# Moving a residual from identity matmuls on TensorE to an addition on VectorE, fed by DMA crossbar transposes

## Chip, cores and metric

The kernel runs on 1 core of one Trainium2 chip. The metric is the device time of one launch in microseconds (us), lower is better. Each time is a median of several executions. Verdicts compare executions of the same state ("fast"); an execution over 1.5% above the fastest of its kernel is called "slow" and left out of a verdict, except where I say otherwise.

## The reference

The input is x, 8 batches of 3136 tokens of 256 channels. A global filter (real FFT over the tokens, product with a complex filter, inverse FFT) is followed by a mixer:

```python
y  = irfft(rfft(x, axis=1) * (filt_r + 1j * filt_i), n=3136, axis=1)
u  = y + (y^T @ U @ V)^T             # low rank (32) over the tokens
out = u + relu(u @ w_ch1) @ w_ch2    # 256 -> 1024 -> 256 channels
```

The change concerns the "u +" of the last line.

## The kernel before

The FFT of length 3136 = 64 x 49 is done as two stages of matmuls each way, in fp16, with intermediate results (ct1, ct2) written to and read from device memory. The batches are worked in five units: 0 and 1 have one batch, 2 to 4 have two. A unit passes through f1 (first stage: x loads, matmul, cast to asb, store to ct1), mid (second stage: a2 loads, matmul pz, filter product uv on VectorE, matmul pe, cast to esb, store to ct2), load_e2, low_rank and then groups of 512 tokens, 6 for each of units 0 and 1 and 12 for each of the others (48), plus one shorter group for each unit. While the groups of one unit run, f1 and mid of the next units are dealt between their steps. Instruction order on each engine is chosen by a scheduler when the kernel is built; each engine and each DMA queue then runs in that order.

A group first makes u with the channels on the partitions (`ut`), because that is what the next matmul needs as its input. The output wants tokens on the partitions, so `ut` must be transposed to be added. Before, this is done by two more matmuls for each 128 tokens, which add into the PSUM tile of the product with w_ch2:

```python
def stage4(gr):
    ...                                        # cut: matmuls into pu
    nc.vector.tensor_copy(gr.ut, pu)           # [128, 2, 512] fp16, channel-major

def residual(gr, o, t0, n):
    for dh in range(2):
        nc.tensor.matmul(o[:, dh * 128:dh * 128 + 128], gr.ut[:, dh, t0:t0 + n], idn,
                         start=False, stop=(dh == 1), skip_group_check=True)

def mm2_part(gr, t):
    ...                                        # cut: the shorter last group
    for tt in range(4 * half, 4 * half + 4):
        nc.tensor.matmul(o, gr.h[tt][:, i * 128:(i + 1) * 128], w2sb[:, tt * DM:(tt + 1) * DM],
                         start=(tt == 0), stop=False, skip_group_check=True)
    if half:
        residual(gr, o, i * 128, 128)
    if t % 4 == 3:
        ...                                    # cut
        nc.vector.tensor_copy(dst, gr.pc.rearrange("p (b j d) -> p b j d", b=u.nb, j=u.jc))

def mirror_filters(a, z):                      # 2 x 808 KB, SBUF to SBUF, at the end of unit 0's mid
    nc.sync.dma_start(fab[0:NR, 1, a:z, :], fab[NR:98, 0, a:z, :])      # NR = 49 partitions
    nc.sync.dma_start(fab[NR:98, 1, a:z, :], fab[0:NR, 0, a:z, :])
```

Loads of x and stores of asb (from unit 1 on) go out on the GpSimd queue, nearly everything else on the sync queue.

## Time and profile before

| | before |
|---|---|
| median of 3 executions | 636.09 us (633.97 to 637.58) |
| span of the profiled execution | 630.4 us |
| PE / VectorE / ScalarE busy | 90% / 51% / 53% |

From the profile's page of the kernel before: busy time of each engine (us, share of the span, instructions), the chain of waits by engine, and the groups of the identity matmuls and of the VectorE copy (busy us, mean ns of one).

```profile
PE 567.5 (90%) x4161; PEld 404.9 (64%) x4161; DVE 323.1 (51%) x376; ACT 332.1 (53%) x618; POOL 83.2 (13%) x136
...
PE 76%; DMA 18%; ACT 2%; SPq 1%; issue 1%; DVE 1%; POOL 0%; ACTq 0%; POOLq 0%
...
L551 DVE COPY och<-pc 128x512 f32<-128x512 f32 x96 | 66.2, 690 | 148.4 <-PE pc L513 131.7
...
L513 PE MATMUL pc<-idn,ut 128*128 128x128 f16 x394 | 55.0, 219 | 0.0
```

The 219 ns are the length of one pipelined matmul, not what it costs. The timeline of PE (start us, length us) shows the cost:

```profile
530.12 0.27 PE L541 MATMUL pc<-w2sb,h_6256 128*128 128x256 f16 x1
530.23 0.28 PE L513 MATMUL pc<-idn,ut 128*128 128x128 f16 x2
530.35 0.60 PE L497 MATMUL phh<-ut,w1sb 128*128 128x512 f16 x2
```

The two identity matmuls start at 530.23 and the next instruction at 530.35, so a pair costs 0.11 to 0.12 us of PE, and a group with its four pairs about 0.44 us.

The next view gives, for stretches of 20 us of the kernel before, the busy us of each engine, then the granted TensorE clock, the busy share of the DMA engines and GB/s.

```profile
80.00:100.00 20.00, 18.64 (x96) 10.55 (x95) 6.72 (x6) 10.57 (x18) 4.82 (x9) 0.79 0.85 193
100.00:120.00 20.00, 15.79 (x120) 11.01 (x119) 9.63 (x13) 9.77 (x19) 9.44 (x16) 1.00 0.98 240
...
160.00:180.00 20.00, 15.90 (x135) 11.09 (x134) 10.78 (x11) 6.96 (x13) 0.00 (x0) 1.00 0.85 218
180.00:200.00 20.00, 19.81 (x116) 12.10 (x115) 17.09 (x15) 13.40 (x25) 0.00 (x0) 1.00 0.65 180
...
560.00:580.00 20.00, 20.00 (x162) 15.32 (x161) 5.91 (x7) 11.60 (x21) 0.00 (x0) 1.00 0.22 59
```

From 80 to 180 us the DMA engines are 85 to 98% busy and PE has gaps. Later PE is full and DMA has room on the whole, but not everywhere: from 240 to 260 us, just before unit 2's groups, the DMA engines are 90% busy again. The chain of waits in the early part runs through transfers (start us, length us):

```profile
109.64 8.58 DMA a_848<-ct_1
...
136.26 13.15 DMA ct_1<-esb
```

### The profile page before, as it was taken

The page shows a single profiled execution, that of the slowest core. Times are in us where ns is not written, and L with a number is a line of the kernel's source. Part 1 is how long each engine was busy: PE and PEld are TensorE (multiplying, and loading weights), DVE is VectorE, ACT ScalarE, POOL GpSimd, SP SyncE. Part 2 cuts the span into 40 slices and gives each one's busy share as a digit, 9 for nine tenths or more (in the row PEclk, how much of TensorE's full clock was granted, in tenths as well). Part 3 has the DMA queues.
Part 4 walks back from the last instruction along what each step waited for, and adds up shares of the span by engine and source line. Part 5 has one row for each costly group of instructions (what it writes and reads, how often), then busy time and mean ns, then how long its engine had stood idle before and what let it go on. Part 6 is the DMA issues. An engine that isn't in the chain of part 4 may idle for free.

```text
span 630.4 us, 10659 instructions
## 1 busy us (share of the span) xinstructions
PE 567.5 (90%) x4161; PEld 404.9 (64%) x4161; DVE 323.1 (51%) x376; ACT 332.1 (53%) x618; POOL 83.2 (13%) x136
## 2 busy tenths in 40 slices
PE   3178289799899999999999999999999999999995
PEld 0166146556556656667677677776777777777774
DVE  5165125676478853337777643476777223233231
ACT  0033046466366656464666665556565555555552
POOL 4230524314100113120001110100000000000000
PEclk9975569999999999999999999999999999999999
DMA  9797689999965579775437685826242753123033
GB/s 164 187 229 185 134 187 220 236 239 218 211 211 154 130 182 285 199 175 144 130 103 174 145 222 190 216 79 185 78 123 75 156 156 101 37 65 101 1 101 109
DMA packets 51993, 98.28 MB, mean 156 GB/s; under 512 B 7386, under 2 KB 29816, under 8 KB 51746
## 3 DMA queue, kind: packets, MB, share of 16 engines
q1 hardware_dynamic: 38742, 69.23, 40.0%
q0 software_dynamic: 11232, 27.20, 21.4%
q10 hardware_dynamic: 1968, 1.17, 0.7%
q8 instruction: 32, 0.52, 0.4%
q14 instruction: 19, 0.16, 0.1%
HBM read 59.88 MB, written 51.38 MB: 177 GB/s over the span
## 4 chain that ended last, share of the span: by engine, by line
PE 76%; DMA 18%; ACT 2%; SPq 1%; issue 1%; DVE 1%; POOL 0%; ACTq 0%; POOLq 0%
PE phh L497 24%; PE pc L541 23%; PE pe L347 8%; PE pz L379 5%; PE pu L482 3%; PE pu L488 3%; PE pc L513 3%; DMA ct_1<-esb 3%; DMA e_2424<-ct_2 3%; PE pf L285 2%; DMA a_342<-ct_0 2%; SPq L420 1%; DMA a_848<-ct_1 1%; DMA a_217<-ct_0 1%; DMA e_540<-ct_0 1%; DMA tf_77<-tf 1%
## 5 line engine op out<-in xcount | busy, mean ns | idle before, releaser
L497 PE MATMUL phh<-ut,w1sb 128*128 128x512 f16 (+2 forms) x848 | 245.8, 369 | 1.8 <-DVE ut L491 1.3
L394 DVE TENSOR_TENSOR uv<-pz,fab 98x1024 f16<-98x1024 f32 (+1 forms) x132 | 141.8, 1087 | 47.6 <-PE pz L379 46.1
L551 DVE COPY och<-pc 128x512 f32<-128x512 f32 x96 | 66.2, 690 | 148.4 <-PE pc L513 131.7
L358 ACT CAST esb<-pe 98x512 f16<-98x512 f32 (+1 forms) x160 | 79.9, 501 | 97.0 <-PE pe L347 78.4
L497 PEld LDWEIGHTS <-w1sb 128*128 128x128 f16 x848 | 105.9, 145 | 31.6 <-issue 8.9
L347 PE MATMUL pe<-uv,g_80 98*98 98x512 f16 (+1 forms) x330 | 90.3, 361 | 1.2 <-DMA g_80<-g 1.2
L491 DVE CAST ut<-pu 128x1024 f16<-128x1024 f32 x48 | 58.7, 1224 | 36.9 <-PE pu L488 36.0
L347 PEld LDWEIGHTS <-g_80 98*98 98x98 f16 x330 | 44.5, 138 | 18.3 <-issue 4.7
L513 PE MATMUL pc<-idn,ut 128*128 128x128 f16 x394 | 55.0, 219 | 0.0
L156 POOL DMA_DIRECT2D x<-in_x_dram x48 | 26.2, 558 | 181.4 <-PE pf L285 169.8
L379 PEld LDWEIGHTS <-tf_77 98*98 98x98 f16 x165 | 22.6, 137 | 32.8 <-issue 21.5
L513 PEld LDWEIGHTS <-ut 128*128 128x128 f16 x394 | 38.5, 98 | 6.8 <-issue 0.8
L290 DVE CAST asb<-pf 128x1024 f16<-128x1024 f32 x21 | 25.6, 1221 | 19.6 <-PE pf L285 18.8
L387 DVE TENSOR_TENSOR uv<-pz,fab 98x512 f16<-98x512 f32 x33 | 22.6, 691 | 12.5 <-PE pz L384 12.1
L285 PE MATMUL pf<-x,wf_64 128*128 128x512 f16 x84 | 25.7, 379 | 0.1
L288 ACT CAST asb<-pf 128x1024 f16<-128x1024 f32 x21 | 21.3, 1012 | 4.7 <-PE pf L285 4.2
L379 PE MATMUL pz<-a_168,tf_77 98*98 98x256 f16 x4 | 1.6, 406 | 14.7 <-DMA a_168<-ct_0 14.3
L433 PEld LDWEIGHTS <-ut_96 128*32 128x32 f16 x120 | 3.1, 101 | 16.0 <-DMA e_537<-ct_0 8.8
L305 POOL DMA_DIRECT2D ct_4<-asb x12 | 8.3, 700 | 36.2 <-ACT asb L288 36.2
L305 POOL DMA_DIRECT2D ct_2<-asb x12 | 8.5, 713 | 29.5 <-ACT esb L358 25.8
L358 ACT ACT_TABLE_LOAD x1 | 1.3, 1283 | 20.2 <-DMA ct_0<-asb 20.2
L285 PEld LDWEIGHTS <-wf_64 128*128 128x128 f16 x84 | 7.4, 98 | 4.3 <-issue 1.6
(1477 smaller groups left out, 1122.3 us busy)
## 6 DMA issues: line engine op xcount, KB each, us to landing
out_dram<-och SPq DMA_DIRECT2D x96, 192.0 KB
x<-in_x_dram POOLq DMA_DIRECT2D x48, 256.0 KB, 7.3
out_dram<-och SPq DMA_DIRECT2D x16, 384.0 KB
ct_2<-asb POOLq DMA_DIRECT2D x12, 256.0 KB, 6.5
ct_3<-asb POOLq DMA_DIRECT2D x12, 256.0 KB, 6.3
ct_4<-asb POOLq DMA_DIRECT2D x12, 256.0 KB, 5.6
ct_2<-esb SPq DMA_DIRECT2D x15, 196.0 KB
ct_3<-esb SPq DMA_DIRECT2D x15, 196.0 KB
```

The lines of the kernel that those rows point to most:

```text
L156: nc.gpsimd.dma_start(t[64 * p:64 * p + 64], dram(x.tensor, (u.b[0] * SEQ + 8 * c) * DM + st * p, [[NR * DM, 64], [1, 8 * DM]]))
L285: nc.tensor.matmul(pf[:, i, :], wf1, u.x[c][:, r:r + 2, :], start=True, stop=True)
L290: nc.vector.tensor_copy(dst, pf)
L347: nc.tensor.matmul(pe[0:98, 0:bd], g3[:, (2 * k + l) * 98:(2 * k + l + 1) * 98], uv[:, l * bd:(l + 1) * bd], start=(k != 32 and l == 0), s ...
L358: nc.scalar.copy(st["esb"][:, i, :], pe[0:98, 0:bd])
L379: nc.tensor.matmul(pz[0:98, 0:bd], wz, a2[c][:, i, :], start=True, stop=True)
L394: nc.vector.tensor_mul(uv.rearrange("p (f b d) -> p f b d", f=2, b=nb), zin, fin)
L491: nc.vector.tensor_copy(gr.ut, pu)
L497: nc.tensor.matmul(ph[:, 0:n], w1v[:, dh, :, t], gr.ut[:, dh, 0:n], start=(dh == 0), stop=(dh == 1))
L513: nc.tensor.matmul(o[:, dh * 128:dh * 128 + 128], gr.ut[:, dh, t0:t0 + n], idn, start=False, stop=(dh == 1), skip_group_check=True)
L541: nc.tensor.matmul(o, gr.h[tt][:, i * 128:(i + 1) * 128], w2sb[:, tt * DM:(tt + 1) * DM], start=(tt == 0), stop=False, skip_group_check=True)
L551: nc.vector.tensor_copy(dst, gr.pc.rearrange("p (b j d) -> p b j d", b=u.nb, j=u.jc))
```

## The change

The intent is to take the identity matmuls off PE, the busiest engine, and to use DMA and VectorE, which have room on average. A crossbar transpose (a DMA that transposes the data on its way) on the sync queue makes a token-major fp16 copy of `ut` (256 KB, SBUF to SBUF), and the VectorE copy out of PSUM, which had to be done anyway, becomes an addition.

```diff
         nc.vector.tensor_copy(gr.ut, pu)
 
+        gr.u16 = sb.tile([128, 2, 4, 128], F16, tag="u16", bufs=2, name="u16")
+        nc.sync.dma_start_transpose(gr.u16.rearrange("p h i d -> p (h i) d"),
+                                    gr.ut.rearrange("p h t -> p (h t)"))
@@ mm2_part
-                             start=(tt == 0), stop=False, skip_group_check=True)
-        if half:
-            residual(gr, o, i * 128, 128)
+                             start=(tt == 0), stop=(tt == 7), skip_group_check=True)
@@ (cut)
-            nc.vector.tensor_copy(dst, gr.pc.rearrange("p (b j d) -> p b j d", b=u.nb, j=u.jc))
+            res = gr.u16[:, :, 2 * y:2 * y + 2, :].rearrange("p h i d -> p i h d")
+            nc.vector.tensor_add(dst.rearrange("p b j (h d) -> p (b j) h d", h=2),
+                                 gr.pc.rearrange("p (i h d) -> p i h d", i=2, h=2), res)
```

## The prediction

> **What bounds the kernel now.** The chain of waits is 76% PE, 18% DMA. The table of stretches splits the span. From 80 to 170 us the 16 DMA engines are 85 to 98% busy and the chain passes through transfers (8.6 us for a2 from ct_1 at 109.6 us, 13.2 us for ct_1 from esb at 136.3). From about 180 us on PE is 98 to 100% busy in nearly every 20 us at clock 1.00, while DMA falls to 13-30% in the last 100 us. Early time is DMA latency, late time is PE issue.
>
> **Removed.** 384 of 394 identity matmuls (the last groups keep theirs). The group list's 219 ns each is pipelined length; in the timeline at 530 to 547 us a pair takes 0.11 us of PE, 0.055 us each: 384 x 0.055 = 21 us; the chain's 3.1% (20 us) agrees. About 50 lie before 180 us, mostly hidden behind DMA; the other 330 are 18 us on the critical path.
>
> **Changed on VectorE.** The 96 copies of 128x512 from PSUM (690 ns) become additions with an SBUF operand. The existing tensor_tensor of 98x512 from PSUM takes 691 ns, so I expect 690 to 720 ns: under 3 us in all, on an engine 51% busy.
>
> **Added.** 48 crossbar transposes of 256 KB, SBUF to SBUF, on the sync queue between the loads and stores that feed the chain. Their source rows are 256 B; packets of 256 B in this trace took 18 ns, so an estimate is 1024 x 18 ns / 16 = 1.2 us of all engines. The Trainium skill, "DMA: Bandwidth & Descriptors", Latency and other measured facts, gives 261 GB/s for a transpose with a non-contiguous middle dimension: estimate 1.0 us. "VectorE: DVE Perf Modes", The three transpose paths, gives 1309 ns for one 128x128 block; eight in series would be 10.5 us, a pessimistic estimate. No trace here shows which yet.
>
> **Deadlines.** stage4 of a group comes every 8.3 us in the tail. Two u16 buffers let a transpose start 1 to 2 us after ut is written; the first addition comes some 11 us later. A landing within 5 us is hidden. In the first unit it is not: the transposes queue behind the two 808 KB mirror copies of the filters (issued 79.8 and 80.8 us), on busy engines. I expect first additions some 3 us later, VectorE, which runs in order, holding back the asb casts, and so a2 loads of unit 1. Seven transposes before 170 us add 8 us of DMA time. Cost early: 5 to 8 us. Later blocking on the sync queue (waits for ut ahead of stores of esb): 2 to 3 us.
>
> **Sum.** 636 - 18 + 7 + 2 = 627, call it 626 us. Range 612 to 648. Faster by over 2% (under 623.4): 0.34; within 2%: 0.47; slower: 0.19.
>
> **What would show each step.** PE: 384 matmuls fewer, and groups in 520 to 620 us every 7.8 to 7.9 us instead of 8.3. VectorE: the addition's mean near 700 ns. DMA: issue to landing of u16 under 5 us in the tail, few waits of och on u16 after 260 us; before 170 us such waits of several us in all. The PE-saturated part starts 5 to 8 us later than before.
>
> **What would make it wrong.** A transpose that takes near 10 us, or stops other traffic while it runs: then additions wait on u16, PE waits for pc, and the result is 650 us or more. The sync queue being held while a transpose is issued, so that a2 and e2 loads come late. Or the opposite: transposes cost nothing in the DMA-bound part, and the whole 20 us comes through (616 us).

## More of the kernel before

A landmark that exists once in each unit is the ScalarE cast of its low-rank sum, after which its groups begin. I use it throughout to cut the span into five stretches: "unit 0 to unit 1" is the time from unit 0's cast to unit 1's, and so on; the last stretch runs to the end. The view is that of the cast's line; "first and last start" is its time.

```profile
L440 ACT CAST h_588<-ph x1: 372/372/372, 79.2 to 79.2; 128x256 f16<-128x256 f32 x1
L440 ACT CAST h_1603<-ph x1: 372/372/372, 174.5 to 174.5; 128x256 f16<-128x256 f32 x1
L440 ACT CAST h_2673<-ph x1: 586/586/586, 257.5 to 257.5; 128x512 f16<-128x512 f32 x1
L440 ACT CAST h_4428<-ph x1: 586/586/586, 387.1 to 387.1; 128x512 f16<-128x512 f32 x1
L440 ACT CAST h_6087<-ph x1: 586/586/586, 513.0 to 513.0; 128x512 f16<-128x512 f32 x1
```

## The result

| | before | after |
|---|---|---|
| median, 4 executions each | 635.98 us | 657.36 us (655.35 to 660.32) |
| ratio | | 1.0342 (95%: 1.029 to 1.0393) |
| span of the profiled execution | 630.4 us | 653.6 us |

A ratio here is the mean time of one kernel's fast runs over that of the other's of the same rounds, so it is not quite the ratio of the medians that I quote. The result is correct, and 3.4% slower; 626 us had been predicted.

The lines of the page after that answer to those shown of before, and a group of the new addition from the list of VectorE's groups:

```profile
PE 555.3 (85%) x3777; PEld 389.8 (60%) x3777; DVE 322.6 (49%) x376; ACT 331.0 (51%) x618; POOL 83.3 (13%) x136
...
PE 70%; DMA 23%; DVE 2%; ACT 2%; SPq 2%; issue 1%; POOL 0%; ACTq 0%; DVEq 0%; POOLq 0%
```

```profile
L554 DVE TENSOR_TENSOR och<-pc,u_1282 128x512 f32<-128x512 f32 x2 | 1.4, 693 | 2.5 <-PE pc L545 2.5
```

PE has 4161 - 3777 = 384 matmuls fewer, as intended, and the addition costs what the copy cost (693 against 690 ns). The loss is elsewhere. The casts of the low-rank sums after:

```profile
L440 ACT CAST h_588<-ph x1: 372/372/372, 79.6 to 79.6; 128x256 f16<-128x256 f32 x1
L440 ACT CAST h_1581<-ph x1: 372/372/372, 205.9 to 205.9; 128x256 f16<-128x256 f32 x1
L440 ACT CAST h_2615<-ph x1: 585/585/585, 287.5 to 287.5; 128x512 f16<-128x512 f32 x1
L440 ACT CAST h_4298<-ph x1: 585/585/585, 419.7 to 419.7; 128x512 f16<-128x512 f32 x1
L440 ACT CAST h_5885<-ph x1: 585/585/585, 543.0 to 543.0; 128x512 f16<-128x512 f32 x1
```

| stretch (us) | before | after | difference | removed matmuls alone would give |
|---|---|---|---|---|
| start to unit 0 | 79.2 | 79.6 | +0.4 | 0 |
| unit 0 to unit 1 | 95.3 | 126.3 | +31.0 | -2.7 |
| unit 1 to unit 2 | 83.0 | 81.6 | -1.4 | -2.7 |
| unit 2 to unit 3 | 129.6 | 132.2 | +2.6 | -5.3 |
| unit 3 to unit 4 | 125.9 | 123.3 | -2.6 | -5.3 |
| unit 4 to end | 117.4 | 110.6 | -6.8 | -5.3 |

(The last column is 0.44 us times 6 or 12 groups.) All of the loss, and more, is in one stretch. In the tail, where PE is full and DMA has room, the change does what it was meant to do: the transposes go out every 7.8 us, while the matmuls of the same place in each group (stage4) came every 8.3 us before. Timeline of PE before, then of the sync queue after:

```profile
530.78 0.39 PE L482 MATMUL pu<-s_78,e_5814 128*128 128x128 f16 x4
...
539.10 0.39 PE L482 MATMUL pu<-s_78,e_5817 128*128 128x128 f16 x4
...
547.41 0.39 PE L482 MATMUL pu<-s_78,e_5817 128*128 128x128 f16 x4
```

```profile
580.45 1.23 SPq L494 DMA_TRANSPOSE u_6307<-ut  x1
...
588.27 1.23 SPq L494 DMA_TRANSPOSE u_6405<-ut  x1
...
596.11 1.23 SPq L494 DMA_TRANSPOSE u_6499<-ut  x1
```

The stretches of 20 us after:

```profile
80.00:100.00 20.00, 16.61 (x96) 10.46 (x96) 6.39 (x7) 12.07 (x19) 5.38 (x10) 0.96 1.07 179
100.00:120.00 20.00, 6.31 (x35) 4.23 (x35) 2.46 (x4) 0.36 (x1) 4.27 (x7) 0.57 1.06 145
...
160.00:180.00 20.00, 16.18 (x93) 11.53 (x92) 8.64 (x12) 9.21 (x22) 5.26 (x10) 0.74 1.04 168
180.00:200.00 20.00, 10.17 (x49) 6.06 (x50) 7.26 (x8) 3.45 (x6) 0.00 (x0) 0.74 0.95 192
...
560.00:580.00 20.00, 20.00 (x158) 15.38 (x157) 7.12 (x9) 11.94 (x20) 0.00 (x0) 1.00 0.47 109
```

From 100 to 120 us PE works 6.3 us in place of 15.8. The DMA engines show more busy time (1.06 in place of 0.98) and move less (145 in place of 240 GB/s): their packets take longer. (The share adds up the time of all packets; packets that overlap can bring it over 1.) PE's granted clock, 1.00 before, is 0.57 and 0.74.

The chain of waits after names a culprit at once, a second one later:

```profile
83.05 29.88 DMA u_607<-ut
112.95 0.70 DVE och L554
...
271.78 15.65 DMA u_2418<-ut
```

The first transpose takes 29.9 us from its issue to the addition that waits for it. VectorE, which runs in order, stands idle for 15.7 us before that addition, and PE behind it, from 98.0 to 113.7 us. VectorE's timeline, the first copy before and the first addition after:

```profile
95.64 0.68 DVE L551 COPY och<-pc 128x512 f32<-128x512 f32 x1
```

```profile
112.95 1.29 DVE L554 TENSOR_TENSOR och<-pc,u_607 128x512 f32<-128x512 f32 x2 [15.74 <-DMA u_607<-ut]
```

And the sync queue is held while it issues transposes (the view of the transpose's line; the middle figure of the three is the ns that an issue took):

```profile
L494 SPq DMA_TRANSPOSE u_607<-ut x1: 7785/7785/7785, 83.0 to 83.0; - x1
L494 SPq DMA_TRANSPOSE u_647<-ut x1: 14947/14947/14947, 91.0 to 91.0; - x1
...
L494 SPq DMA_TRANSPOSE u_1282<-ut x1: 10616/10616/10616, 155.9 to 155.9; - x1
...
L494 SPq DMA_TRANSPOSE u_2418<-ut x1: 10438/10438/10438, 271.8 to 271.8; - x1
...
L494 SPq DMA_TRANSPOSE u_3479<-ut x1: 1232/1232/1232, 361.7 to 361.7; - x1
```

An issue takes 1.2 us in a quiet stretch; of the six in unit 0 to unit 1, four take 5 to 15 us. In the records of single DMA packets, the 1024 pieces of 256 B of one transpose pass within 1.4 us in the tail, the last 2.6 us after the issue began; those of the first are spread over some 20 us. They start at 87.2 us, stop at 89.2 and go on at 98.2, when the mirror copies end. Near the first, eight packets of x loads (4096 B, usually 322 ns) took 10.6 to 11.0 us each, from 88.7 us on; before, no packet of this size took over 2.4 us.

So there are three suspects for one stretch: VectorE standing in order behind a late u16; a crossbar transpose that holds up other transfers; and simply 256 KB more for each group in a place where the DMA engines are full. The chain alone cannot tell, since it follows only the wait that ended last.

### The profile page after: what moved, and what is told of

Read it like the earlier page. It is cut to its first block, busy times and chain, and to the rows that moved or that the text cites. A ratio compares the mean times of both kernels' runs of the same rounds, so it can differ in the third digit from the quotient of the medians.

```text
span 653.6 us, 9996 instructions
## 1 busy us (share of the span) xinstructions
PE 555.3 (85%) x3777; PEld 389.8 (60%) x3777; DVE 322.6 (49%) x376; ACT 331.0 (51%) x618; POOL 83.3 (13%) x136
## 4 chain that ended last, share of the span: by engine, by line
PE 70%; DMA 23%; DVE 2%; ACT 2%; SPq 2%; issue 1%; POOL 0%; ACTq 0%; DVEq 0%; POOLq 0%
PE phh L501 23%; PE pc L545 22%; PE pe L347 8%; PE pz L379 5%; DMA u_607<-ut 5%; PE pu L482 3%; PE pu L488 3%; DMA u_2418<-ut 2%; PE pf L285 2%; DMA a_1167<-ct_1 2%; DMA a_342<-ct_0 2%; DMA ct_1<-esb 1%; DMA a_217<-ct_0 1%; DMA e_540<-ct_0 1%; DMA tf_77<-tf 1%; DMA ct_0<-al 1%
## 5 line engine op out<-in xcount | busy, mean ns | idle before, releaser
L501 PEld LDWEIGHTS <-w1sb 128*128 128x128 f16 x848 | 112.2, 145 | 33.6 <-issue 6.3
L347 PEld LDWEIGHTS <-g_80 98*98 98x98 f16 x330 | 45.4, 140 | 24.9 <-issue 10.4
L379 PEld LDWEIGHTS <-tf_77 98*98 98x98 f16 x165 | 23.4, 142 | 42.7 <-issue 18.3
L545 PE MATMUL pc<-w2sb,h_689 128*128 128x256 f16 x4 | 1.3, 334 | 15.7 <-DVE och L554 15.7
L379 PE MATMUL pz<-a_1597,tf_77 98*98 98x512 f16 x4 | 2.3, 577 | 10.8 <-DMA a_1597<-ct_2 10.8
L318 ACT CAST al<-pf 128x256 f16<-128x256 f32 (+1 forms) x4 | 1.5, 368 | 17.5 <-PE pf L312 17.5
```

Source lines behind the costliest of these rows:

```text
L347: nc.tensor.matmul(pe[0:98, 0:bd], g3[:, (2 * k + l) * 98:(2 * k + l + 1) * 98], uv[:, l * bd:(l + 1) * bd], start=(k != 32 and l == 0), s ...
L379: nc.tensor.matmul(pz[0:98, 0:bd], wz, a2[c][:, i, :], start=True, stop=True)
L501: nc.tensor.matmul(ph[:, 0:n], w1v[:, dh, :, t], gr.ut[:, dh, 0:n], start=(dh == 0), stop=(dh == 1))
```

## The experiments

All ran on one core against the kernel before. "Stretch" below is unit 0 to unit 1 in the run's profile (one execution). In the runs where unit 0 has nothing added this stretch is 95.3, 96.6, 96.6, 97.9, 98.1, 99.4 and 100.9 us, so I take 95 to 101 us as undisturbed. (The 100.9 is from a profile of the slow state, of units 2 to 4 below; without it the range ends at 99.4.) Single profiles scatter elsewhere too: the time before unit 0's cast, which no experiment was to change, is 73.8 to 82.2 us. So I compare stretches, not spans, and in this stretch take no difference under some 5 us in one profile for an effect.

### Transposes that nobody reads

The kernel before with the 48 transposes added:

```diff
         nc.vector.tensor_copy(gr.ut, pu)
+        gr.u16 = sb.tile([128, 2, 4, 128], F16, tag="u16", bufs=2, name="u16")
+        nc.sync.dma_start_transpose(gr.u16.rearrange(...), gr.ut.rearrange(...))
```

> The kernel before (identity matmuls, copies) plus the 48 transposes, whose result nobody reads. Measure: the time from the cast of the low-rank sum of unit 0 to that of unit 1 (95.3 us before, 126.3 us after), and the ratio to before. Theory X (a crossbar transpose that meets busy DMA engines stalls traffic and holds the sync queue): the loss stays without any reader, interval 112 to 128 us, ratio 1.03 to 1.06, with x packets of 4096 B that take over 5 us. Rival S (the loss is VectorE standing in order behind the wait for u16): interval under 103 us, ratio under 1.015.

Measured: correct, 672.12 us (one of the four executions slow), ratio 1.0585 (1.0537 to 1.0633); stretch 126.6 us, against 126.3 with the reader. VectorE's timeline in this run:

```profile
96.03 0.68 DVE L555 COPY och<-pc 128x512 f32<-128x512 f32 x1
...
101.16 0.69 DVE L555 COPY och<-pc 128x512 f32<-128x512 f32 x1 [1.45 <-PE pc L517]
...
112.17 1.22 DVE L290 CAST asb<-pf 128x1024 f16<-128x1024 f32 x1 [7.07 <-DMA ct<-asb]
```

The first two copies out of PSUM come at 96.0 and 101.2 us (95.6 and 100.8 before), so VectorE no longer waits for a transpose. It is held at 112.2 us all the same, by a store of asb that is late, and the chain now runs through x loads, stores of ct and loads of a2:

```profile
122.11 15.47 DMA a<-ct
```

Rival S falls as the whole cause: taking away the 15.7 us wait that stood on the chain gives back nothing, so the loss needs no reader. It does not follow that the wait was harmless in the kernel after, since the two equal stretches are made up differently. PE's long gap is from 98.0 to 113.7 us there, behind the addition, and from 119.0 to 137.6 us here, until loads of a2 land. The first matmul pz of unit 1 starts 34.7 us after unit 0's cast before, 47.2 after and 58.2 here; the rest of the stretch is 60.6, 79.1 and 68.4 us.

### A plain copy in the place of the transpose, read

```diff
-        nc.sync.dma_start_transpose(gr.u16.rearrange("p h i d -> p (h i) d"),
-                                    gr.ut.rearrange("p h t -> p (h t)"))
+        nc.sync.dma_start(gr.u16.rearrange("p h i d -> p (h i) d")[:, :, 0:128],
+                          gr.ut.rearrange("p h (i d) -> p (h i) d", d=128))   # u16 rows padded to 144
```

> The kernel after with each transpose replaced by a plain copy of the same 256 KB on the same queue, at the same place, written in runs of 256 B, read by the same additions. The result is wrong on purpose. Theory X (it is the crossbar transpose's own behaviour under load): interval unit 0 to unit 1 back to 96 to 106 us, no x packet over 5 us, sync queue held about 0.6 us an issue, ratio to before 0.965 to 0.995. Rival Q (any transfer of that size in that place of the queue would do it: first in, first out behind the mirror copies, and 12.6 MB more in 256 B pieces): interval 115 us or more, ratio 1.02 or more.

Measured: 645.81 us, ratio 1.0173 (1.0114 to 1.0231), result wrong as intended; stretch 115.8 us. The first copy still lands 27.1 us after its issue, though no packet of x takes over 2 us and an issue holds the queue for 0.65 us. VectorE still waits for it:

```profile
110.21 1.29 DVE L554 TENSOR_TENSOR och<-pc,u 128x512 f32<-128x512 f32 x2 [10.83 <-DMA u<-ut]
```

The stretch is what rival Q expected, the ratio just under it. But about a third of the loss goes with the crossbar, which Q had not; the rest stays.

### A plain copy that nobody reads

The unread form of the last, in the kernel before.

> Fourth corner of a square: transpose or plain copy, read or unread. Read transpose (after): interval unit 0 to unit 1 126.3 us; unread transpose 126.6; read copy 115.8; this is the unread copy, in the kernel before with its identity matmuls. Theory X2 (two separate ways to lose the same stretch: VectorE waits in order for a u16 that lands late whatever moves it, and crossbar transposes delay the x, ct_1 and a2 transfers; each alone is enough): with both removed the interval is 95 to 101 us, ratio to before 0.995 to 1.015. Rival Q (12.6 MB more in 256 B pieces on full engines costs the time by itself): interval 106 us or more, ratio 1.02 or more.

Measured: correct, 652.58 us, ratio 1.0292 (1.0257 to 1.0327); stretch 113.6 us. My theory of two separate causes (X2) falls, and rival Q has it: a plain, unread copy costs 18 us here against the profile of before, 13 against the upper end of the undisturbed range. PE stands idle from 110.2 to 123.9 us; its longest gap there was 3.0 us before. The first load of a2 is issued 33.7 us after unit 0's cast (30.0 before), and it takes 12.0 us on the chain, where that of the chain before took 8.58:

```profile
111.83 12.03 DMA a<-ct
```

The square is now full:

| stretch unit 0 to unit 1 (us) | read by the addition | unread |
|---|---|---|
| crossbar transpose | 126.3 | 126.6 |
| plain copy | 115.8 | 113.6 |
| nothing added | | 95.3 |

By these single profiles any such copy costs about 18 to 20 us (13 at the least, against the undisturbed range), and being a crossbar transpose another 10 to 13 us. Being read changes the sum by -0.3 and +2.2 us, but this comparison is not clean: the read kernels also lack the identity matmuls (2.7 us in this stretch at most), and by the traces PE, ScalarE and VectorE work in another order in them soon after 92 us. In the unread kernels these engines keep the order of before through the whole stretch; only the sync queue's differs in the plain copy's, from 155.7 us on. So the column on the right is the one to rest on.

### The plain, unread copy with an eighth of the bytes

```diff
-        nc.sync.dma_start(gr.u16...[:, :, 0:128],   gr.ut...)          # 256 KB
+        nc.sync.dma_start(gr.u16...[:, 0:1, 0:128], gr.ut...[:, 0:1])  # 32 KB
```

> The unread plain copy (interval unit 0 to unit 1 113.6 us) cut to one eighth, 32 KB in place of 256 KB, so that nearly the same instructions stand in nearly the same order on every queue, with an eighth of the bytes. If the bytes on full engines cost the 18 us: interval 95 to 101 us, ratio to before 1.00 to 1.01. If it is the extra entries of the sync queue (their waits ahead of other transfers) or the new order of instructions that the scheduler chose: interval still 108 us or more, ratio 1.02 or more.

Measured: correct, 639.20 us, ratio 1.0079 (1.0043 to 1.0116); stretch 101.6 us, just above the undisturbed range. With the same number of entries on the sync queue, their waits and nearly the same order of instructions, 12 of the 18 us are gone. So most of it is the bytes, or the pieces that they come in, on full engines. A late landing by itself is not the cost: the first of these small copies also lands only 18.9 us after its issue.

### The mirror copies cut so that they can use more engines

I had thought that the first transpose starts on the DMA engines that the 49-partition mirror copies leave free, and waits there for the others. (In the trace, the last steps of a mirror copy's completion semaphore are 7 single ones; after the cut, a copy of 48 has 16.)

```diff
-        nc.sync.dma_start(fab[0:NR, 1, a:z, :], fab[NR:98, 0, a:z, :])
-        nc.sync.dma_start(fab[NR:98, 1, a:z, :], fab[0:NR, 0, a:z, :])
+        for p, n in ((0, 48), (48, 1)):
+            nc.sync.dma_start(fab[p:p + n, 1, a:z, :], fab[NR + p:NR + p + n, 0, a:z, :])
+            nc.sync.dma_start(fab[NR + p:NR + p + n, 1, a:z, :], fab[p:p + n, 0, a:z, :])
```

In the kernel after:

> The kernel after with each mirror copy of 49 partitions cut in 48 + 1, so that it can spread over 16 engines in place of 7. Theory X (the first transpose starts on the engines that the mirror copies leave free and waits there, blocking x loads, until the 7 others are done): the first transpose lands within 12 us of its issue (29.9 us after), no x packet over 5 us near it, interval unit 0 to unit 1 shorter by 10 to 18 us (108 to 116), ratio 1.00 to 1.02. Rival Q (plain queueing behind 1.6 MB at full DMA load): the same bytes are still ahead of it, landing over 18 us, interval over 120 us, ratio over 1.025.

Measured: correct, 656.53 us, ratio 1.0322 (1.0243 to 1.0402). The profiled execution was slow, so I use it only for what is far larger than that: the first transpose lands 29.4 us after its issue, as before the cut, and the stretch is 131.2 us. Only the very long packets are gone (one over 5 us in place of ten, and that one at 143 us). So the long x packets are not what makes the stretch long, and this form of theory X falls.

In the kernel before, as the control:

> Control for the last: the kernel before with the same cut of the mirror copies. Every theory expects little, since nothing there waits for the mirror copies until unit 1's filter products: interval 93 to 97 us, ratio 0.99 to 1.01.

Measured: correct, 630.91 us, ratio 0.9942 (0.9908 to 0.9976); stretch 96.6 us. The cut alone is worth half a per cent; its profile does not show where, since its stretches lie within 1.5 us of those of before.

### The mirror copies on another queue

```diff
-        nc.sync.dma_start(fab[...], fab[...])      # both mirror copies
+        nc.scalar.dma_start(fab[...], fab[...])
```

> The kernel after with the two mirror copies issued from ScalarE's queue in place of the sync queue, so that the first transposes no longer stand behind them in one queue. If standing behind them (first in, first out) makes the first transpose late: it lands within 12 us of its issue (29.9 us after) and VectorE's 15.7 us wait for it goes. If sharing busy engines with the x loads and the mirror copies makes it late: still over 20 us. Either way, since the unread transpose lost the same stretch (126.6 us against 126.3), I expect the interval unit 0 to unit 1 to fall by less than the landing does: 112 to 125 us, ratio to before 1.01 to 1.03.

Measured: correct, 661.54 us. Two of the four executions were slow (665.4 and 666.1; the others 649.9 and 657.7), so I do not rest on its ratio of 1.0467, which is above what I expected; the mean of the two fast ones, 653.8 us, is 1.03 times that of the runs of before beside it. In its profile (a fast one) the stretch is 120.4 us; the first transpose is issued at 81.3 us and the addition that needs it starts at 106.8 us, over 25 us later, with no mirror copy ahead of it in its queue. So queueing behind them is not what makes it late. From 92 to 96 us, while the mirror copies ran on the other queue, the packet records show only some 120 of the transposes' pieces of 256 B, with a mean of about 400 ns and a median of 31, where 18 is usual; after the mirror copies ended (97.6 us) the pieces came faster.

### Where transposes are used

The remaining four choose by unit or group, and use identity matmuls elsewhere. All have this edit, with another condition:

```diff
+    def use_xbar(gr):
+        return gr.u.n >= 1            # or: >= 2; == 4; the condition of the last
...
+        if use_xbar(gr):
             gr.u16 = ...; nc.sync.dma_start_transpose(...)
...
+        if half and not use_xbar(gr):
+            residual(gr, o, i * 128, 128)
...
+            if use_xbar(gr): nc.vector.tensor_add(...)  else: nc.vector.tensor_copy(...)
```

Units 1 to 4:

> Unit 0 keeps identity matmuls and copies, units 1 to 4 use the transposes. Theory X2: all of the loss of after came from unit 0's six transposes, so the interval unit 0 to unit 1 is 94 to 99 us, the others stay as in after (81.6, 132.2, 123.3, 110.6), ratio to before 0.98 to 0.995. If transposes of later units cost as much as those of unit 0, the ratio stays over 1.00.

Measured: correct, 632.62 us, ratio 0.9982 (0.9936 to 1.0028); stretch 99.4 us, the others 85.7, 131.9, 123.9 and 110.9. Six transposes in unit 0 are the whole difference between 1.034 and 0.998. The ratio is a little above the range I gave, by 4 us in unit 1 to unit 2, which I have not explained.

Units 2 to 4:

> Units 0 and 1 as before, units 2 to 4 with transposes (36 of 48). Saves 288 of 384 identity matmuls, 288 x 0.055 = 16 us of PE. Full gain would be ratio 0.975. Theory X2 with a clock that stays high (no long PE idle): 0.975 to 0.985. If the later stretches keep a DMA-bound part of their own (unit 2 to 3 lost 2.6 us in after in place of gaining 5), 0.985 to 0.995.

Measured: correct, 631.18 us, ratio 0.9921 (0.9877 to 0.9966), the second of the two expectations. Its profile was slow, so I read nothing more from it.

The same with the mirror copies cut in 48 + 1:

> The last with the mirror copies cut in 48 + 1 as well, which alone gave 0.994. If the two are independent: the last one's ratio less 0.004 to 0.008, that is 0.968 to 0.985, the fastest so far.

Measured: correct, 626.89 us, ratio 0.9884 (0.9839 to 0.993), less gain than the range expected. (From the ratio of the last, 0.9921, less 0.004 to 0.008, it is about what two independent gains give.) Its profile is of the slowest of its six executions, 5 us above their median. Its stretches are 96.6, 83.1, 137.6, 123.1 and 110.8: unit 2 to unit 3 lost 8 us where 5 should have been gained. The chain there:

```profile
278.66 12.88 DMA ct<-al
291.66 3.94 DMA a<-ct
```

and VectorE's timeline:

```profile
291.62 0.69 DVE L563 TENSOR_TENSOR och<-pc,u 128x512 f32<-128x512 f32 x1 [13.59 <-DMA u<-ut]
```

The last store of unit 3's first stage takes 12.9 us; in the kernel before the same store was issued at 276.9 us and the load that needs it could go at 279.3 us. The sync queue issued transposes at 268.3 and 278.1 us (2.9 and 3.7 us each), an addition waited 13.6 us for one of them, and PE was busy 0.36 of the 8 us from 288 to 296. This is a second place of the same kind: the start of unit 2's groups meets the end of unit 3's first stage, with its x loads and stores. Both waits end at 291.6 us, and no run takes them apart; how much a usual execution loses here, this slowest one cannot say.

Unit 4 alone:

> Transposes in unit 4 alone (12 of 48), everything else as before, mirror copies as before. Saves 96 matmuls: 5.3 us. Every theory expects the last stretch to fall from 117.3 to about 111 us and the others to stay: ratio 0.988 to 0.993. It measures what an unobstructed transpose is worth per group: about 0.5 us.

Measured: correct, 627.28 us (two of the six executions slow), ratio 0.9905 (0.986 to 0.9949); the last stretch is 112.1 us. That is the gain of 12 unobstructed groups, 5.3 us or 0.44 us a group by this profile.

Only groups with no first-stage or e2 traffic beside them:

```diff
+        return (gr.u.n == 4 or gr.u.n == 3 and gr.g >= 2
+                or gr.u.n == 2 and 3 <= gr.g <= 7)          # with the mirror copies cut in 48 + 1
```

> Transposes only in groups with no x loads, first-stage stores or e2 loads in flight by the trace of before: unit 2 groups 3 to 7, unit 3 from group 2 on, unit 4; 27 of 48; with the mirror copies cut in 48 + 1. Saves 216 identity matmuls, 216 x 0.055 = 12 us. If transposes off the busy stretches are free: 631 - 12 = 619, ratio to before 0.970 to 0.982, stretches 96.6, 83, 126 to 129, 122 to 125, 110 to 111 us. If they also cost there: ratio over 0.988.

Measured: correct, 623.14 us (618.78 to 629.50, one of the six slow), ratio 0.9823 (0.9785 to 0.9862), at the upper edge of what I expected, and the fastest of all. Stretches 98.1, 83.2, 127.4, 123.7 and 110.7. Its 27 transposes each hold the queue for 1.2 to 2.2 us:

```profile
L499 SPq DMA_TRANSPOSE u<-ut x27: 1232/1232/2167, 290.9 to 598.5; - x27
```

It beats both kernels, though with an interval that reaches across the line of 2%, so that its verdict is "unclear" and not "faster". (Its profile is of its fastest execution, and 5 us of that one's lead lie before unit 0's cast.) Against the control with the cut alone (0.9942) the transposes themselves give about 1.2%, some 7 us (the two ran in different calls), where 216 matmuls at 0.055 us are 12 us.

## Why the prediction was wrong

- **Removed work: right.** 384 matmuls less, 0.055 us each. In the tail a group takes 7.8 us in place of 8.3, as predicted; the last stretch gained 6.8 us.
- **The addition costs what the copy did: right.** 693 ns, predicted 690 to 720.
- **A quiet transpose is short and hidden: right.** The pieces pass in 1.4 us (estimate 1.2), the last 2.6 us after the issue began, well under the 5 us limit. The unread transposes left the last stretch at 116.8 us (117.4 before): in the tail they are free. The pessimistic 10.5 us did not apply there.
- **The term that failed is "Cost early: 5 to 8 us"** (with "Seven transposes before 170 us add 8 us of DMA time"). The stretch unit 0 to unit 1 lost 31 us. I had priced a transfer on full engines at the time of its packets on free engines. The runs show in its place 13 to 20 us for six plain copies of 256 KB there, 12 of them gone with seven eighths of the bytes, and 10 to 13 us more because they are crossbar transposes. My own list of what would make it wrong had named a transpose that stops other traffic, and 650 us or more for it; I gave it too little weight.
- **The reason I gave for it failed too.** I expected that first additions come late, and that VectorE then holds back the asb casts. They do come late, by 17 us rather than 3 (112.95 us against 95.64), and the chain shows it; but with nobody waiting for u16 the stretch was just as long. Nor was it the place behind the mirror copies in the sync queue that made the transpose late: with them on another queue the landing still took over 25 us.
- **"Later blocking on the sync queue: 2 to 3 us" was too small as well.** In units 2 and 3 the expected 10.6 us of gain came to nothing (+2.6 and -2.6). Part of that is the collision at the start of unit 2. The rest of it in unit 3 to unit 4, where 5.3 us were due and 2 to 3 came in every run with transposes read, I have not settled.
- **A loss that I had not priced at all: the clock.** The Trainium skill, "TensorE: Matmul & The Clock Gate", What's actually happening, says that the clock is either half or full, and drops to half after one idle window of about 3.4 us. The trace agrees: its clock records hold only 0.5 and 1.0, and the half-clock pieces after 100 us last 17.1, 10.2, 10.2, 6.8 and 6.8 us, and each begins in a gap of PE of 3.6 us or more (the longest gap of the kernel before after 100 us, 3.0 us, brought none). In them matmuls of 512 columns start every 426 ns, elsewhere every 216. From 100 us to shortly before the end, the kernel before spent none of its time at half clock, the kernel after 51 us. A wait of PE is thus paid a second time in the work after it. No run varies the clock alone, so how much of the 31 us it makes is open.

What stays open in the early stretch: why 1.5 MB more (six copies), about 8 us at the 200 GB/s moved there, cost 13 to 20 us. It is not throughput alone: with the unread copies, the DMA engines move only 8 GB/s from 124 to 128 us, just after the late loads of a2. The skill's "DMA: Bandwidth & Descriptors", Queues, rings and completion order, says that an engine goes round its queues packet by packet; then small packets of one queue could stand behind 4096 B packets of another. No run here varied the packet size by itself. For the first plain copies the trace suggests something simpler: of the 16 steps of a copy's completion semaphore 9 come 7 to 10 us after the issue and 7 after 19 to 29 us, and 7 is the number of a mirror copy's own late steps, so seven parts may have stood behind the mirror copies. Nor is it shown by what means crossbar transposes cost their 10 to 13 us. That the first one can hold up x loads is shown by the packets of 10.6 to 11.0 us, which occur in no run with plain copies; but they do not occur with the mirror copies cut or on another queue either, and there the stretch is still 131 and 120 us.

## What to carry to other kernels

In this kernel, moving work from a full engine to DMA was worth its price only where DMA had room at that moment. So read the DMA share stretch by stretch, not the mean of the span, and move the work only in the groups where the stretch is quiet. A transfer's time on free engines says little about its cost on full ones, for itself or for its neighbours. And a long wait on the chain is a suspect, not a verdict: remove the reader and see if the time comes back. If it does not, look at where the engine now stands idle before you call the wait harmless.

## What the Trainium skill lacked or had wrong

- "DMA: Bandwidth & Descriptors", Rules for kernel authors, says: "A transpose next to ordinary DMAs needs nothing". The row is about wrong data, and for the result it held (all runs with transposes were correct). It says nothing of time: beside busy engines a transpose of 256 KB took up to 29.9 us from issue to use, eight packets of another queue that usually take 322 ns took up to 11.0 us, and the stretch lost 10 to 13 us more than with plain copies.
- The same page, DMA Transpose (X-bar), does not say that the issuing queue is held (the page has an issue cost only where it compares with another generation of the chip, and nothing under load): 1.2 us for an issue of 256 KB in quiet stretches, up to 14.9 us in busy ones, against 0.65 us for a plain copy of the same size.
- The same page, Latency and other measured facts, has 261 GB/s for a transpose. Here 256 KB from SBUF to SBUF took 1.4 us from first to last piece in a quiet stretch, 187 GB/s (262,144 B / 1.4 us), and 2.6 us counted from the issue.
- "VectorE: DVE Perf Modes", The three transpose paths, gives 1309 ns for one 128x128 block by the crossbar and no figure for many blocks in one transfer. Eight of them in one took 2.6 us here, so the blocks do not simply add.
